# Linear attention and two MoE layers: eleven first products of block 1 moved into block 0, all stores issued by GpSimd, k, v and q in transfers of 512 KB, four weights converted ahead of block 0

## The chip, the cores and the metric

The kernel runs on one core of a Trainium2 chip. The metric is the device time of one execution in microseconds; the lower is the better. Times of runs are medians; the profile is of one further execution of the same program.

## What is computed

The reference is a linear attention with a root-mean-square norm, followed by two layers of two products each, in float32:

```python
kv  = einsum('bhsd,bhse->bhde', k, v)          # batch 8, heads 8, seq 576, head_dim 64
out = einsum('bhsd,bhde->bhse', q, kv)
x   = out / sqrt(mean(out * out, -1) + 1e-6) * g_norm
x   = x.transpose(0, 2, 1, 3).reshape(4608, 512)
h   = x @ w_in;  r = maximum(h, 0)             # 512 -> 2048
x   = (s * (r * r) + b) @ w_out                # 2048 -> 512
h   = x @ w2_in                                # second layer
y   = (h / (1 + exp(-1.702 * h))) @ w2_out
```

The weights arrive as 64-bit floats and are converted on the core, each into a high and a low float32r part; a product of float32 precision is then three products of 128x128 by 128x512 (high by high, high by low, low by high).

## The kernel before

The 4608 tokens are nine blocks of T = 512; the 512 features are four pairs of heads (NP = 4), two groups of two pairs (NG = 2). The 2048 hidden features are NF = 16 slices of 128. A weight tile is one slice of w_in (`which` 0) or of w_out (`which` 1), 512 KB as it arrives.

For one block j of attention, `kv_product` (L303) makes k'v of a batch on TensorE and `kv_keep` (L320) copies it out on ScalarE; `att_product` (L332) multiplies by q; `att_square` (L349) squares on ScalarE; for block 0 `att_mean`, `att_root`, `att_newton` work per pair of heads, for the other blocks `block_mean` (L392), `block_root`, `block_newton` work for all pairs at once, `y_store` and `y_load` (L410, L415) take the factor through memory to spread it over the partitions, and `att_scale` applies it. `att_split` (L428) makes the high part xh and the low part xl that the first layer reads.

The first layer, for the first three blocks (NPLAIN), is `mlp_h` (L473: twelve matmuls of 128x512, one slice f), `mlp_act` and `mlp_g` (the square of the positive part and its split into gh and gl), and `mlp_o` (L517: twelve matmuls that add slice f into four accumulators). I call such twelve matmuls a group, h(j, f) or o(j, f). The later blocks and the second layer use a scheme with seven products in place of eight (`g1_product`, `g2_product`), with sums of weights that are made once and stored to memory (`a_store`, `wo_store`, `op_store`).

A weight is loaded by `w_load` (L129) and converted in four steps: `w_low` (two ScalarE instructions), `w_words` (four on VectorE, L151 to L158), `w_hi` (one on ScalarE, L168) and `w_lo` (one on VectorE, L173). In block 0 every one of the 32 groups needs a weight of the first layer that has just been converted; blocks 1 and 2 use the same converted weights again.

The order is written by hand: each piece of work is put into a list by `at(slot, ...)`, where one slot is about one group of TensorE, the list is sorted by slot, and every engine gets its instructions in that order. So an instruction that waits holds up all that stands behind it on its engine. Loads and stores are issued by SyncE (SP), but for the `y` transfers, which GpSimd (POOL) issues; a queue too goes by its order. Large tiles come from 42 slots of 4 KB per partition (`big`), smaller ones from 23 of 2 KB (`mid`); PSUM has eight banks.

In the kernel before block 0 starts from a table and a formula for the conversions, and the blocks follow one another, h and o in turn:

```python
START = [(-61, -60, -54, -52, -45), (-59, -54, -53, -47, -42), ...]
weight(-128, -58.5, 3.5, CONV[0], 0, 0, 0)
weight(-89, -48.5, 4, CONV[0], 0, 1, 0)
for n, (f, w) in enumerate(...):
    weight(n - (5 if n < 12 else 4), n - 1, 1, CONV[1], 0, f, w)
for j in range(NPLAIN):
    plain(0, j, 32 * j, j == NPLAIN - 1)
```

## Time and profile before

| | |
|---|---|
| runs | 1566.7 us median of three, 1566.52 to 1568.53 |
| profiled execution, its own time | 1564.6 us |
| its span in the trace | 1562.8 us |
| mean granted TensorE clock | 0.992 of 2.4 GHz |
| busy: TensorE, weight loads | 1533.9 us (98%), 1235.5 us (79%) |
| busy: VectorE, ScalarE, GpSimd | 1063.9 us (68%), 795.4 us (51%), 40.3 us (3%) |
| DMA | 392.11 MB, 251 GB/s in the mean |

The profiled execution is 2.1 us below the median of the runs, and 1.8 us of its time lie outside the span. A matmul's busy time in the trace overlaps the next one's, so a busy TensorE is not one at its peak: how much it does is seen from the starts of its instructions. Names of engines in the rows: PE is TensorE, PEld its weight loads, DVE VectorE, ACT ScalarE, POOL GpSimd, SPq the queue of SyncE. A row of the timeline is start, duration, engine, line, operation, tiles and shape, number of instructions, and in brackets how long the engine had been idle before it and what ended that.

### The profile page before, as it was taken

How to read it: one execution, taken by the hardware profiler on the slowest of the kernel's cores; microseconds unless marked ns; L12 is line 12 of the kernel's file. 1: busy time of each engine (PE TensorE's matmuls, PEld its weight loads, DVE VectorE, ACT ScalarE, POOL GpSimd, SP SyncE). 2: the span in 40 equal slices, each digit the busy share in tenths (PEclk: the TensorE clock that was granted, in tenths of full speed). 3: DMA queues.
4: the chain of work that ended last, by engine and by line, in shares of the span. 5: the costliest groups of instructions: out<-in, count | busy, mean ns of one | idle time of the engine just before them, and what ended most of it. 6: DMA issues, size and time to landing. Idle time of an engine off the chain costs nothing.

```text
span 1562.8 us, 20560 instructions
## 1 busy us (share of the span) xinstructions
PE 1533.9 (98%) x7316; PEld 1235.5 (79%) x7316; DVE 1063.9 (68%) x1535; ACT 795.4 (51%) x1169; POOL 40.3 (3%) x84
## 2 busy tenths in 40 slices
PE   6999999999999999999999999999999999999998
PEld 4767777887788777888888888888888888888887
DVE  5997355566787468956761779678968896778422
ACT  4987455445696368934881335324522453244222
POOL 0010110101100011000000000000000000000000
PEclk8999999999999999999999999999999999999999
DMA  9463759869897889959770947884788478646670
GB/s 302 156 223 119 246 187 346 305 213 329 290 360 244 303 302 346 323 181 386 269 274 8 361 178 280 292 301 167 270 314 302 164 264 283 231 146 222 225 295 28
DMA packets 175527, 392.11 MB, mean 251 GB/s; under 512 B 23041, under 2 KB 54785, under 8 KB 175425
## 3 DMA queue, kind: packets, MB, share of 16 engines
q1 hardware_dynamic: 172096, 382.27, 69.7%
q0 software_dynamic: 3328, 8.52, 1.8%
q8 instruction: 58, 0.95, 0.2%
q14 instruction: 45, 0.36, 0.1%
HBM read 300.42 MB, written 90.31 MB: 250 GB/s over the span
## 4 chain that ended last, share of the span: by engine, by line
PE 84%; DVE 7%; issue 3%; DMA 3%; ACT 3%; SPq 0%; POOL 0%; DVEq 0%; ACTq 0%; POOLq 0%
PE o L524 26%; PE o L695 19%; PE h L481 8%; PE d L567 8%; PE a L567 8%; PE b L567 4%; PE f L567 4%; PE c L567 4%; DVE cu L157 1%; DVE w L173 1%; DMA yb<-yd 1%; PE kv L312 1%; DMA qq<-in_q 1%; PE o_ps L343 1%; DVE ca L158 1%
## 5 line engine op out<-in xcount | busy, mean ns | idle before, releaser
L524 PE MATMUL o<-gh,w 128*128 128x512 f32 x1280 | 406.8, 391 | 0.8 <-ACT gh L505 0.4
L524 PEld LDWEIGHTS o<-gh,w 128*128 128x128 f32 x1280 | 240.0, 188 | 56.6 <-issue 3.1
L695 PE MATMUL o<-gh,wl 128*128 128x512 f32 x896 | 276.5, 389 | 0.0
L524 PE MATMUL o<-gl,w 128*128 128x512 f32 x640 | 249.3, 390 | 0.4 <-DVE gl L514 0.2
L695 PEld LDWEIGHTS o<-gh,wl 128*128 128x128 f32 x896 | 168.2, 188 | 34.9
L481 PE MATMUL h<-xh,w 128*128 128x512 f32 x512 | 174.3, 402 | 4.0 <-DVE xh L442 2.7
L695 PE MATMUL o<-gl,wl 128*128 128x512 f32 x448 | 174.3, 389 | 0.0
L567 PE MATMUL d<-xh,wl 128*128 128x512 f32 x448 | 157.2, 391 | 7.0 <-DVE r L593 7.0
L567 PE MATMUL a<-xh,wl 128*128 128x512 f32 x448 | 157.5, 392 | 0.0
L524 PEld LDWEIGHTS o<-gl,w 128*128 128x128 f32 x640 | 120.1, 188 | 25.9 <-DVE gl L514 1.5
L481 PEld LDWEIGHTS h<-xh,w 128*128 128x128 f32 x512 | 98.1, 192 | 33.2 <-issue 3.5
L583 ACT ACTIVATE c<-a 128x512 f32<-128x512 f32 x56 | 33.4, 597 | 166.3 <-PE a L567 163.4
L567 PEld LDWEIGHTS d<-xh,wl 128*128 128x128 f32 x448 | 84.1, 188 | 27.8 <-DVE r L593 9.6
L481 PE MATMUL h<-xl,w 128*128 128x512 f32 x256 | 101.7, 397 | 0.0
L567 PEld LDWEIGHTS a<-xh,wl 128*128 128x128 f32 x448 | 84.5, 189 | 20.4 <-issue 1.9
L695 PEld LDWEIGHTS o<-gl,wl 128*128 128x128 f32 x448 | 84.1, 188 | 17.5
L638 DVE TENSOR_TENSOR gl<-r,gh 128x512 fp32r<-128x512 f32 x96 | 65.2, 688 | 39.0 <-PE o L524 23.1
L669 ACT ACTIVATE gh<-t 128x1024 fp32r<-128x1024 f32 x48 | 51.0, 1063 | 72.5 <-DVE t L660 62.4
L567 PE MATMUL a<-xl,wl 128*128 128x512 f32 x224 | 87.6, 391 | 0.0
L567 PE MATMUL d<-xl,wl 128*128 128x512 f32 x224 | 87.2, 389 | 0.0
L622 ACT ACTIVATE r<-r 128x1024 f32<-128x1024 f32 x84 | 84.6, 1052 | 0.0
L674 DVE TENSOR_TENSOR gl<-r,gh 128x1024 fp32r<-128x1024 f32 x64 | 77.3, 1221 | 6.9 <-ACT gh L669 6.9
(116 smaller groups left out, 2520.2 us busy)
## 6 DMA issues: line engine op xcount, KB each, us to landing
wl<-wsd SPq DMA_DIRECT2D x168, 512.0 KB, 7.0
wl<-wo2S SPq DMA_DIRECT2D x64, 512.0 KB, 5.7
wsd<-op SPq DMA_DIRECT2D x96, 256.0 KB, 4.7
w<-wod SPq DMA_DIRECT2D x48, 512.0 KB, 6.9
wl<-wo2A SPq DMA_DIRECT2D x48, 512.0 KB, 4.6
raw<-in_w_in SPq DMA_DIRECT2D x32, 512.0 KB, 7.9
raw<-in_w_out SPq DMA_DIRECT2D x32, 512.0 KB, 8.0
wl<-wsd SPq DMA_DIRECT2D x56, 256.0 KB, 6.3
```

The source lines that it names most:

```text
L157: dve.scalar_tensor_tensor(out=t, in0=raw[:, :, 1], scalar=SIGN_TOP, in1=t, op0=ALU.bitwise_and, op1=ALU.bitwise_or)
L158: dve.tensor_tensor(out=q, in0=t, in1=q, op=ALU.add)
L173: dve.tensor_sub(out=w[:, 1, :], in0=q.bitcast(F32), in1=w[:, 0, :].bitcast(F32))
L481: pe.matmul(h, lhsT=a, rhs=b, start=(n == 0), stop=(n == 3 * NP - 1))
L524: pe.matmul(acc[m, j][c], lhsT=a, rhs=x, start=(f == 0 and n == 0), stop=(f == NF - 1 and n == 2))
L567: pe.matmul(o, lhsT=a, rhs=b, start=(first and n == 0), stop=(n == 5), skip_group_check=not first)
L583: act.activation(st["c1"], st[0], AF.Copy)
L622: act.activation(R[q, n], R[q, n], fn)
L638: dve.tensor_sub(out=gl, in0=R[q, i][:, half, :], in1=gh.bitcast(F32))
L669: act.activation(hi, src, AF.Copy)
L674: dve.tensor_sub(out=lo, in0=src, in1=hi.bitcast(F32))
L695: pe.matmul(so[k, d], lhsT=a, rhs=b, start=(first and n == 0 and i == 0 and e == 0), stop=(n == 3 and i == 1 and e == 2), skip_group_check ...
```

## The change

The start is written out event by event (BEGIN), in place of START and its formulas. The first four slices of w_in (f 0 to 3) are loaded and converted there, and h(0, 0), h(0, 1) and h(0, 2) are cut in two: the half that needs the first two pairs of heads goes first (`mlp_h` has `first` and `last`). Dummy matmuls (`fill`) stand between them. `plan()` writes the order of the groups of blocks 0 to 2: eight h of block 0 first, then each o of block 0 followed by one h of block 0 or by one or two h of block 1, so that eleven h of block 1 stand in block 0; blocks 1 and 2 overlap likewise. The attention of block 1 moves to the start of block 0 (ATT). Weights are loaded 7.5 slots ahead of their group in place of 4 or 5 slots ahead of their conversion. All stores, the first q tiles, the constants and most of the tails of k and v (`tail_load`) are issued by GpSimd. k and v of a pair come in one transfer, q of a group in one transfer in place of two or four. `big` has 41 slots, `mid` 25.

```diff
-START = [(-61, -60, -54, -52, -45), (-59, -54, -53, -47, -42), (-54, -48, -48, -43, -41), (-50, -49, -46, -40, -36)]
-KV = ((1, 5), (20, 27), (34, 41), (46, 57), (62.5, 66.5), (74, 79), (84, 89))
-CONV = [(0, 1, 2, 3), (-0.5, 0, 1, 1.5)]
-NBIG, NMID = 42, 23
+KV = ((-0.5, 2.5), (24.5, 28), (34, 41), (46, 57), (62.5, 66.5), (74, 79), (84, 89))
+CONV = (-1.75, -1, 0.5, 1.0)
+BEGUN = 4
+LOAD = 7.5
+ATT = ((1.5, 2.5, 3.3), (40, 3.5, 4.8), (55, 4, 4.8), (67, 4, 4.8))
+LEAD_G = 3.9
+SIDE = (0, 0, 0, 1, 2, 0, 0, 0, 0, 2, 0, 1, 1, 1, 1, 2)
+BEGIN = [
+    (-0.1, 'tail', 0), (0.7, 'qp', 0, 0), (0.8, 'kv', 0, 0), (0.8, 'w', 0, 0, 0), (1, 'kv', 0, 1), (1.2, 'kv', 0, 2), (1.5, 'kv', 0, 3),
+    (1.6, 'w', 0, 1, 0), (1.7, 'w', 0, 2, 0), (1.8, 'w', 0, 3, 0), (2.0, 'qp', 0, 1), (6, 'kvp', 0, (0,), True, False), (6.25, 'fill', 2),
...
+    (25.8, 'hi', 0, 3, 0), (26.1, 'lo', 0, 2, 0), (26.1, 'lo', 0, 3, 0), (26.3, 'h', 0, 0, 0, 0, 2), (27.1, 'split', 0, 2),
+    (27.9, 'fill', 4), (28.3, 'split', 0, 3), (28.51, 'fill', 2), (28.71, 'fill', 4), (29.5, 'h', 0, 0, 1, 0, 2),
+    (32, 'h', 0, 0, 2, 0, 2),
+]
+def plan():
+    out = [("h", 0, f, *((2,) if f < 3 else ())) for f in range(8)]
+    ahead = 0
+    for i, n in enumerate(SIDE):
+        out += [("o", 0, i)]
+        if n:
+            out += [("h", 1, ahead + k) for k in range(n)]
+            ahead += n
+        else:
+            out += [("h", 0, 8 + sum(not k for k in SIDE[:i]))]
+    for i in range(NF - ahead):
+        out += [("o", 1, i), ("h", 1, ahead + i)]
...
+NBIG, NMID = 41, 25
     def wo_store(f):
-        nc.sync.dma_start(out=wod[f], in_=W[0, f, 1].bitcast(F32))
+        pool.dma_start(out=wod[f], in_=W[0, f, 1].bitcast(F32))
...
         for a, name in enumerate(OP_PAIRS[which][k]):
-            nc.sync.dma_start(out=op_place(m, i, which, name), in_=t[:, a, :].bitcast(F32))
+            pool.dma_start(out=op_place(m, i, which, name), in_=t[:, a, :].bitcast(F32))
...
     def kv_load(b, p):
-        kvin[b, p] = new2(F32, "k_in"), new2(F32, "v_in")
-        for n, t in enumerate(kvin[b, p]):
-            nc.sync.dma_start(out=t.rearrange("q (c d) -> q c d", c=4), in_=kv_h[b, p, :, n])
+        t = kvin[b, p] = new(big, [P, 2, 4, P], F32, "kv_in")
+        nc.sync.dma_start(out=t, in_=kv_h[b, p])
...
-    def q_load(j, g):
-        qin[j, g] = [new2(F32, "qq") for _ in range(2)]
-        for h, qq in enumerate(qin[j, g]):
-            for o, n, b, s in segments(j):
-                nc.sync.dma_start(out=qq[:, o:o + n], in_=q_h[b, g, :, h, s:s + n])
+    def q_load(j, g, queue=nc.sync):
+        qin[j, g] = new4(F32, "qq")
+        queue.dma_start(out=qin[j, g], in_=q_h[j, g])
...
-            nc.sync.dma_start(out=xd[0][j][p], in_=x)
+            pool.dma_start(out=xd[0][j][p], in_=x)
...
-    def mlp_h(m, j, f):
+    def mlp_h(m, j, f, first=0, last=NP):
...
-            nc.sync.dma_start(out=out[c * P:(c + 1) * P, j * T:(j + 1) * T], in_=t)
+            pool.dma_start(out=out[c * P:(c + 1) * P, j * T:(j + 1) * T], in_=t)
...
+    order = plan()
+    for n, (kind, j, f, *part) in enumerate(order):
+        slot = n - 0.005
+        if kind == "h":
+            at(slot, mlp_h, 0, j, f, *part)
+            at(slot + 1, mlp_act, 0, j, f)
+        else:
+            g = max(slot - LEAD_G, [e[:3] for e in order].index(("h", j, f)) + 1.01)
+            at(g, mlp_g, 0, j, f)
+            at(slot, mlp_o, 0, j, f)
...
+        if j == 0 and (kind == "o" or f >= BEGUN):
+            which = int(kind == "o")
+            at(n - LOAD, w_load, 0, f, which)
+            for i, fn in zip(CONV, (w_low, w_words, w_hi, w_lo)):
+                at(n - 4 + i, fn, 0, f, which)
...
-    for j in range(NPLAIN):
-        plain(0, j, 32 * j, j == NPLAIN - 1)
...
-    for j, slot in zip(range(1, NPLAIN + 2), (10, 35.5, 49, 66)):
-        attend(j, slot, 4, 4.8)
+    for j, slots in zip(range(1, NPLAIN + 2), ATT):
+        attend(j, *slots)
```

From the second slice of block 3's seven products on, the order on TensorE, VectorE and ScalarE is the same as before, instruction by instruction, but for some copies of block 2's sums, which stand a few places earlier; SP and POOL differ up to the end.

On TensorE, at the end of a group o(0, f) in block 0, before. A tile's number tells which one it is: xh_340 is block 0's operand, w_687 a weight converted just ahead.

```order
L524 MATMUL o_551<-gh_664,w_652 128x512
L524 MATMUL o_551<-gl_665,w_652 128x512
L524 MATMUL o_551<-gh_664,w_652 128x512
L481 MATMUL h_810<-xh_340,w_687 128x512
L481 MATMUL h_810<-xl_341,w_687 128x512
L481 MATMUL h_810<-xh_340,w_687 128x512 x2
L481 MATMUL h_810<-xl_341,w_687 128x512
```

The same engine with the change, at the end of o(0, 3). Here w_284 is the slice f 0 of w_in, already used for block 0, and xh_825 block 1's operand.

```order
L575 MATMUL o_769<-gh_851,w_862 128x512
L575 MATMUL o_769<-gl_852,w_862 128x512
L575 MATMUL o_769<-gh_851,w_862 128x512
L528 MATMUL h_964<-xh_825,w_284 128x512
L528 MATMUL h_964<-xl_826,w_284 128x512
L528 MATMUL h_964<-xh_825,w_284 128x512 x2
L528 MATMUL h_964<-xl_826,w_284 128x512
```

Before, every group of block 0 takes a new weight; now eleven groups that need no new weight stand between those that do.

On VectorE, in the start, before: the splits of pairs 1 to 3 (xh, xl) and the second weight's conversion.

```order
L442 CAST xh_340<-x0_331 128x512
L443 TENSOR_TENSOR xl_341<-x0_331,xh_340 128x512
L443 TENSOR_TENSOR xl_355<-x0_350,xh_354 128x512
L370 SCALAR_TENSOR_TENSOR y2_336<-ms_333,y2_336 128x512
L371 SCALAR_TENSOR_TENSOR y_335<-y2_336,y_335 128x512
L382 SCALAR_TENSOR_TENSOR x0_362<-o_ps_307,g_col_70,y_335 128x512
L173 TENSOR_TENSOR w_358<-ca_312,w_358 128x512
L443 TENSOR_TENSOR xl_355<-x0_362,xh_354 128x512
```

VectorE with the change, up to the splits of pairs 2 and 3 (that of pair 1 stands four rows ahead of the first).

```order
L217 TENSOR_TENSOR w_353<-ca_324,w_353 128x512
L195 TENSOR_SCALAR cu_350<-cu_350 128x512
L196 TENSOR_SCALAR cu_350<-cu_350 128x512
L201 SCALAR_TENSOR_TENSOR cu_350<-raw_212,cu_350 128x512
L202 ISA ca_349<-cu_350,ca_349 128x1024
L217 TENSOR_TENSOR w_370<-ca_345,w_370 128x512
L217 TENSOR_TENSOR w_383<-ca_349,w_383 128x512
L487 TENSOR_TENSOR xl_395<-x0_343,xh_394 128x512
L487 TENSOR_TENSOR xl_395<-x0_374,xh_394 128x512
```

The splits of pairs 2 and 3 now stand behind four converted weights, before behind two.

On GpSimd, the transfers of the factor y of block 5 (yd_143) and its neighbours, before.

```order
L412 DMA yd_142<-y 8x512
L418 DMA yb<-yd_142 64x512 x8
L412 DMA yd_143<-y 8x512
L418 DMA yb<-yd_143 64x512 x8
L412 DMA yd_144<-y 8x512
```

GpSimd with the change, around block 5's.

```order
L296 DMA wsd_0_104<-op 128x512 x4
L456 DMA yd_143<-y 8x512
L296 DMA wsd_0_104<-op 128x512 x2
L462 DMA yb<-yd_143 64x512 x2
L296 DMA wsd_0_104<-op 128x512 x2
L462 DMA yb<-yd_143 64x512 x4
L474 DMA x0d_125<-oc 128x512
L462 DMA yb<-yd_143 64x512 x2
L474 DMA x0d_125<-oc 128x512 x3
```

Stores of weights and of attention rows, which SP issued before, now stand in the same queue as the y transfers and among them. GpSimd issues 412 transfers in place of 72.

## Rows read from the trace of the kernel before

**Rows 1.** Busy time by stretch: window and length, busy and (count) of PE, PEld, DVE, ACT, POOL; PE clock, DMA share, GB/s.

```profile
27.60:46.20 18.60, 15.05 (x74) 10.38 (x73) 15.99 (x28) 14.03 (x26) 0.00 (x0) 0.72 0.85 302
46.20:80.90 34.70, 34.61 (x201) 25.91 (x200) 33.60 (x61) 32.64 (x58) 0.00 (x0) 1.00 0.44 137
80.90:93.10 12.20, 8.77 (x21) 4.29 (x21) 11.74 (x22) 12.04 (x22) 0.00 (x0) 0.72 0.90 282
121.60:139.30 17.70, 16.18 (x92) 10.76 (x91) 16.32 (x30) 15.94 (x29) 0.00 (x0) 1.00 0.21 64
605.00:1560.00 955.00, 953.36 (x4207) 789.07 (x4205) 654.44 (x841) 416.00 (x572) 0.00 (x0) 1.00 0.68 244
```

**Rows 2.** The chain that ended last, in order of time: start, length, what; block 2.

```profile
160.31 2.72 PE h L481 x12
```

**Rows 3.** Timeline of PE, 27 to 412 us.

```profile
27.63 0.90 PE L481 MATMUL h<-xh,w 128*128 128x512 f32 x1
...
46.24 0.39 PE L524 MATMUL o<-gh,w 128*128 128x512 f32 x1
...
49.06 1.15 PE L312 MATMUL kv<-v_in,k_in 128*64 128x64 f32 x32
...
50.36 0.50 PE L481 MATMUL h<-xh,w 128*128 128x512 f32 x1
...
80.91 1.05 PE L397 MATMUL ms<-sq,ones_c 128*32 128x512 f32 x4
84.82 1.05 PE L397 MATMUL ms<-sq,ones_c 128*32 128x512 f32 x2 [2.86 <-ACT sq L352]
...
93.16 0.39 PE L524 MATMUL o<-gh,w 128*128 128x512 f32 x1
...
121.67 0.39 PE L481 MATMUL h<-xh,w 128*128 128x512 f32 x1
...
137.54 0.39 PE L524 MATMUL o<-gh,w 128*128 128x512 f32 x1
...
411.71 1.06 PE L397 MATMUL ms<-sq,ones_c 128*32 128x512 f32 x8
```

**Rows 4.** Timeline of ACT in the start.

```profile
8.73 0.27 ACT L328 ACTIVATE kvs<-kv 64x128 f32<-64x128 f32 x1 [6.70 <-PE kv L316]
...
14.15 0.67 ACT L145 ACTIVATE cu<-raw 128x512 f32<-128x512 f32 x1
```

**Rows 5.** Timeline of DVE: first conversion, then the last step of weights.

```profile
14.85 0.43 DVE L151 TENSOR_SCALAR cu<-cu 128x512 f32<-128x512 f32 x1 [12.24 <-ACT cu L145]
...
44.92 0.68 DVE L173 TENSOR_TENSOR w<-ca,w 128x512 fp32r<-128x512 f32 x1
47.77 0.69 DVE L173 TENSOR_TENSOR w<-ca,w 128x512 fp32r<-128x512 f32 x1
51.23 0.69 DVE L173 TENSOR_TENSOR w<-ca,w 128x512 fp32r<-128x512 f32 x1
...
143.48 0.68 DVE L173 TENSOR_TENSOR w<-ca,w 128x512 fp32r<-128x512 f32 x1
```

**Rows 6.** Timeline of DVE and PE around block 5's factor y.

```profile
391.14 0.75 DVE L423 SCALAR_TENSOR_TENSOR oc<-oc,g_col,yb 128x512 f32<-128x512 f32 x1 [2.73 <-DMA yb<-yd]
401.84 0.50 PE L567 MATMUL d<-xh,wl 128*128 128x512 f32 x1 [2.04 <-DVE r L593]
```

**Rows 7.** Timeline of POOL there.

```profile
385.86 4.30 POOL L418 DMA_DIRECT2D yb<-yd  x8 [4.88 <-ACT cu L145]
```

**Rows 8.** The tile yb: count, duration in ns, least, median and most, first and last start.

```profile
L418 POOL DMA_DIRECT2D yb<-yd x64: 518/526/723, 99.2 to 597.1; - x64
```

**Rows 9.** DMA issues: count, KB each, median us from issue to landing.

```profile
out<-st SPq DMA_DIRECT2D x36, 256.0 KB, 2.5
yb<-yd POOLq DMA_DIRECT2D x64, 128.0 KB, 3.7
```

**Rows 10.** The end: SP's last stores.

```profile
1557.05 2.41 SPq L548 DMA_DIRECT2D out<-st  x4
```

More of the change, by code (lines that the diff above doesn't have):

```diff
@@ new lines, in plan @@
+def plan():
[10 more added lines that the diff above has]
+        out += [("o", 1, i), ("h", 1, ahead + i)]
+    done = 0
+    for i in range(NF - ahead, NF):
+        out += [("o", 1, i)]
+        if (NF - i) % 2:
+            out += [("h", 2, done)]
+            done += 1
+    for i in range(NF - done):
+        out += [("o", 2, i), ("h", 2, done + i)]
+    return out + [("o", 2, i) for i in range(NF - done, NF)]
@@ L211, in w_join, with w_spent @@
         dve.tensor_add(out=q.bitcast(F32), in0=w[:, 0, :].bitcast(F32), in1=w[:, 1, :].bitcast(F32))
+        w_spent(f)
+    spent = set()
+    def w_spent(f):
+        if f in spent:
+            drop(W.pop((0, f, 0)))
+        spent.add(f)
     sums, parts = {}, {}
@@ L309, in kv_product @@
                 for p in units:
[L310 to L311 removed]
+                    r = p % 2 * D
+                    kt_, vt_ = (kvin[b, p][:, n, c, h * D:(h + 1) * D] for n in range(2))
                     pe.matmul(kv[r:r + D, p // 2, h * D:(h + 1) * D], lhsT=kt_, rhs=vt_, start=(p in (opens, opens + 1) and h == 0 and c == 0), stop=False,
@@ L471 @@
     G, acc = {}, {}
-    def mlp_h(m, j, f):
+    def mlp_h(m, j, f, first=0, last=NP):
         x = xT[m, j]
-        h = G[m, j, f] = psum("h")
-        n = 0
-        for c in range(NP):
+        if first == 0:
+            G[m, j, f] = psum("h")
+        h = G[m, j, f]
+        n = 3 * first
+        for c in range(first, last):
+            assert m or (0, j, c) in done
             wh, wlo = (w_part(m, f, 0, i, c) for i in range(2))
@@ L482, in mlp_h @@
                 n += 1
-        if m or j == NPLAIN - 1:
+        if last < NP:
+            return
+        if m:
             drop(W.pop((m, f, 0)))
+        elif j == NPLAIN - 1:
+            w_spent(f)
         if f == NF - 1:
@@ L735, in at @@
         events.append((slot, len(events), fn, a))
-    def weight(load, slot, gap, conv_at, *unit):
-        at(load, w_load, *unit)
-        for i, fn in zip(conv_at, (w_low, w_words, w_hi, w_lo)):
-            at(slot + gap * i, fn, *unit)
-    def attention(slots, j, p):
-        at(slots[0], att_product, j, (p,))
-        for slot, fn in zip(slots, (att_square, att_mean, att_root, att_newton, att_split)):
-            at(slot, fn, j, p)
     def attend(j, slot, gap, late):
         for g in range(NG):
-            at(slot - 4 + g, q_load, j, g)
+            at(slot - 3.2 + g, q_load, j, g)
             at(slot + gap * g, att_product, j, (2 * g, 2 * g + 1))
@@ L875, in x_done, with start, fill @@
         drop(*(xin.pop(k) for k in left))
-    for p in range(NP):
-        at(-99 + p, kv_load, 0, p)
-        if p == 0:
-            at(-98.95, tail_load, 0)
-        at(START[p][0], kv_product, 0, (p,), p == 0, p == NP - 1)
-        at(START[p][0], kv_keep, 0, p)
-        at(-98.9 + p, q_half, p)
-        o, m, n, x = START[p][1:]
-        attention((o, m, m, n, x), 0, p)
-    weight(-128, -58.5, 3.5, CONV[0], 0, 0, 0)
-    weight(-89, -48.5, 4, CONV[0], 0, 1, 0)
-    for n, (f, w) in enumerate([(f - LAG * w, w) for f in range(1, NF + LAG) for w in range(2) if 0 <= f - LAG * w < NF][1:]):
-        weight(n - (5 if n < 12 else 4), n - 1, 1, CONV[1], 0, f, w)
+    warm = cp.tile([P, P], F32, name="warm")
+    idle = psum("idle")
+    def start(t, fn, *a):
+        at(t - 200, fn, *a)
+    def fill(n):
+        for _ in range(n):
+            pe.matmul(idle[:, :P], lhsT=warm, rhs=warm, start=True, stop=True)
+    for t, fn, *a in BEGIN:
+        start(t, {"fill": fill, "kv": kv_load, "q": q_load, "qp": lambda j, g: q_load(j, g, pool), "tail": tail_load, "w": w_load, "kvp": kv_product, "keep": kv_keep, "o": att_product,
+                  "sq": att_square, "mean": att_mean, "root": att_root, "newton": att_newton, "split": att_split, "low": w_low,
+                  "words": w_words, "hi": w_hi, "lo": w_lo, "h": mlp_h}[fn], *a)
+    start(60, drop, idle)
+    order = plan()
[8 more added lines that the diff above has]
+            at(slot, mlp_o, 0, j, f)
+            if j == NPLAIN - 1:
+                at(slot, wo_done, 0, f)
+            if f == NF - 1:
+                at(slot + 0.03, mlp_store, 0, j)
+        if j == 0 and (kind == "o" or f >= BEGUN):
[3 more added lines that the diff above has]
+                at(n - 4 + i, fn, 0, f, which)
     for b, slots in zip(range(1, B), KV):
@@ L987 @@
         act.add_instruction(mybir.InstLoadActFuncSet(name=nc.get_next_instruction_name(), act_func_set_id=6, ins=[], outs=[]))
-        warm = cp.tile([P, P], F32, name="warm")
         dve.memset(warm, 0.0)
-        idle = psum("idle")
-        for _ in range(14):
-            pe.matmul(idle[:, :P], lhsT=warm, rhs=warm, start=True, stop=True)
-        drop(idle)
+        fill(14)
         consts()
         for slot, _, fn, a in events:
+            if slot > STOP:
+                break
             fn(*a)
```

45 lines of the change are left out of this document (24 added, 21 removed).

## The prediction

> **What bounds the kernel now.** I read the windows first, since a busy share over the whole span mixes stages. From 605 to 1560 us TensorE is busy for 953.36 of 955.00 us at full clock [rows 1], and the chain of waits runs through groups of twelve matmuls that take 2.72 us each [rows 2]. The reader is to see that nothing can be gained there: the change leaves that work and its order as they are. So the question is how much TensorE loses before that, above all in block 0 (to 138 us), where each group needs a freshly converted weight.
>
> Busy time doesn't answer it, because a waiting TensorE can look busy; the starts of its instructions do [rows 3]. I set the time between two starts against the groups in between, at 2.72 us each [rows 2], and the product k'v, at 50.36 - 49.06 = 1.30 us [rows 3]. Three stretches lose time:
>
> - A, 27.63 to 46.24 us: 18.61 us for three groups (8.16) and a k'v: 9.15 us lost. The granted clock there is 0.72, a mean over full and half speed (2.4 and 1.2 GHz) [rows 1].
> - B, 80.91 to 93.16 us: 12.25 us for one group and sums of squares worth 1.06 (the row at 411.71): 8.5 us lost. The sums wait 2.86 us for ScalarE's squares [rows 3]; then matmuls run at the half clock, and the mean is again 0.72 [rows 1].
> - C, 121.67 to 137.54 us: 15.87 us for four groups (10.88) and a k'v: 3.7 us lost, at full clock [rows 1, 3].
>
> The cause of A and C is VectorE. One weight costs it 47.77 - 44.92 = 2.85 us; two weights in a row and the low part of a square take 51.23 - 44.92 = 6.31 us [rows 5], while TensorE's pair of groups that uses them takes 5.44 us. From 46.2 to 80.9 us VectorE is busy for 33.60 and ScalarE for 32.64 of 34.70 us [rows 1]. From its first conversion at 14.85 to the end of the last at 144.2 us VectorE has 129 us of work in line with the 32 groups of block 0 [rows 5]: it is the bound of this stage, and TensorE the follower.
>
> **The change, part by part.** The eleven groups h(1, f) cost TensorE nothing new: they are taken out of block 1. They do need block 1's attention sooner, which VectorE and ScalarE now do in the start. What they bring is time for conversions: 43 groups run while 32 weights are converted, so the ratio turns from 6.31 against 5.44 us per pair to about 6.31 against 7.31 (5.44 x 43/32).
>
> Start. Before, ScalarE makes the first low parts at 14.15 us though the copy of the first k'v had ended at 9.00 [rows 4]; now they stand right behind that copy. VectorE's first conversion may start at about 11.5 in place of 14.85 us [rows 4, 5], but two more weights are then converted ahead of the last splits, and the first h waits for splits of pairs 0 and 1. I set it at 26.5 in place of 27.63: **+1 us** of gain, between -1.5 (the extra conversions delay it) and +3 (it follows VectorE's 3.35 us).
>
> A. In place of whole groups, the halves of h(0, 0) to h(0, 2) on pairs 0 and 1 stand ahead, so that TensorE has 4 us of work while pairs 2 and 3 are split. VectorE's work up to the split of pair 3 is four weights less one step (11 us) and some 17 further operations of 0.6 to 0.75 us, 22 to 23 us in all; with the idle share of before (2.6 of 18.60 us [rows 1]) and waits on the first sums, it is done near 38 us. TensorE with its halves and a k'v from 26.5 would be there at 33 to 34. So 4 us of wait, and about 1.5 us at the half clock or between matmuls: 5.5 us lost in place of 9.15, **+3.6**, between 0 (nothing is better) and +9 (all goes).
>
> B. The sums of block 1 still stand some four slots behind the products whose squares they wait for, and ScalarE has the same queue ahead of it. I take half: 4 in place of 8.5, **+4.5**, between 0 and +8.5.
>
> C. At the last weight TensorE has 40 groups, four k'v and block 1's attention behind it: 26.5 + 108.8 + 5.2 + 3 = 144 us, while VectorE, started 3 us earlier, gets there at 141. So TensorE is the bound at the end, and of the 3.7 us I leave 1.7: **+2**, between 0 and +3.7.
>
> A new wait. The eleven groups do not stand evenly: up to o(0, 2) there are eight h in a row and then o and h in turn, each with a new weight, and h(1, 0) comes only behind o(0, 3). VectorE ends the 13th weight at 11.5 + 39 (13 weights of 2.85 and the words of the next) + 18 (three low parts, splits and factors of blocks 0 and 1, 0.6 to 0.75 us each) + 5 of idle time as before = 74 us. TensorE comes to that group at 26.5 + 32.6 (12 groups) + 2.6 (two k'v) + 3 (attention) + 9.5 (what A and B leave) = 74 us. That is even; I put **-1.5** there, between -6 (VectorE is a tenth slower than its sum) and 0.
>
> Stores. 340 transfers move from SP's queue to POOL's. POOL's own issues take 526 ns each [rows 8], so 340 x 0.53 = 180 us on an engine that is busy for 40 of 1563 us: hidden under TensorE, as buffers of stored tiles come free two slots or more before they are needed again. SP has fewer issues and may load earlier; TensorE waits for no load after the start, so 0. If that cover fails, the price is a load late by the length of a queue, some 2 us a piece. Only the last store shows: out<-st lands 2.5 us after issue from SP, yb<-yd 3.7 us from POOL [rows 9], and SP's last four start at 1557.05 [rows 10]. That is **-1.2**, between -2 and 0.
>
> One rule speaks against the stores on POOL. The rows show that 64 yb issues took between 518 and 723 ns, median 526, beside a VectorE that was busy for two thirds of the time [rows 8, 1]: at most 0.2 us of delay each. The Trainium skill ("SBUF — State Buffer", section "Who interferes with whom") says that a transfer issued by GpSimd has its descriptors written by GpSimd, which is shut out while VectorE runs a copy, cast or tensor_scalar in its two-port mode, and so advises another queue. By it each moved store could be held for up to the length of such an instruction; by the rows the hold is 0.2 us at most, 340 x 0.2 = 68 us of POOL's time, still off the path.
>
> k, v and q in fewer, larger transfers carry the same bytes: 0, with SP's saved issues in the same cover. The dummy matmuls fill waits; they can delay the h behind them by their own length, which is inside A's lower bound.
>
> From 139 to 605 us VectorE and TensorE lose some 11 us in the sums for the seven products; the order there is unchanged, and I set it at 0, between -17 (the third rival) and +2.
>
> Sum: 1 + 3.6 + 4.5 + 2 - 1.5 - 1.2 = 8.4 us gained on the profiled execution's own 1564.6: 1556.2. The median of the runs is 2.1 us above that execution, so the median after is about **1558**.
>
> **The rivals.** First, all waits of block 0 go: A's 9.15, B's 8.5 and C's 3.7, less the last store, 20 us at most and some 17 likely, 1549. For it speaks the slack of 43 groups against 32 weights; against it the sums of block 1, which are ordered as tightly as before.
>
> Second, VectorE remains the bound: the lead is used up by the 13th weight, and the waits of A and B come back there with a half clock behind them. It decides if VectorE's sum of 74 us is over by more than a tenth. Then the wait takes 6 us or more and the gain is under 3: 1565. The even finish of the two sums speaks for it, the easier end of block 0 against it.
>
> Third, slower: the y transfers stand behind stores in POOL's queue. Before, POOL waited 4.88 us for block 5's factor and then issued eight yb in 4.30 us [rows 7]; VectorE waited 2.73 us for one of them at 391.14, and TensorE 2.04 us for VectorE at 401.84 [rows 6]. With two stores ahead of each pair, at 0.53 to 1.06 us each [rows 8], pairs land 1.1 to 2.1 us later, some 4.2 us a block over four pairs, in four blocks: 17 us, 1575. It decides once yb lands later than VectorE arrives, and VectorE already waits. Against it: POOL's wait of 4.88 us leaves room for stores ahead of the factor, and later pairs land while VectorE works on the first. The skill's rule above would add to this rival's price and not create it.
>
> That the change doesn't do what it says is excluded by the order: the eleven groups stand where the text says.
>
> **How the numbers follow.** My forecast, 1553 to 1563, has a chance of 0.55; all waits gone 0.20; VectorE still the bound 0.15; slower 0.10. A measurement of this kernel can tell about 0.2%, 3.1 us, from no change, so "same" is 1563.6 to 1569.8. It takes most of the second rival; the third is all of "slower". Faster takes the forecast, the first rival and a little of the second: 0.77, 0.13, 0.10. The range runs from 1547 (first rival, with a better start) to 1566 (second rival); what it leaves out is the third and the outermost of the first.
>
> **What would show it.** In the timeline of TensorE, the first h at 26 to 27 us; three halves and then a wait of about 4 us; the sums of block 1 with a shorter wait ahead of them and less half clock; the stretches A to C together losing some 10 us less; no new wait of TensorE on VectorE between 70 and 86 us of over 3 us. The stretch 345 to 605 should lose no more than before, and VectorE's wait for yb stay near 2.7 us. The forecast is wrong if that wait grows in each block, if TensorE's waits in 60 to 90 us add up to more than before, or if the first h comes later than 29 us.

## The result, and the profile after

The change makes the kernel faster: 1548.04 us median of four runs (1547.74 to 1548.96) against 1567.62 us of four runs of before (1566.52 to 1568.84); ratio 0.9876, 95% interval 0.9859 to 0.9893. Beside the last experiments the changed kernel ran again (e16_after_again, expected at 1547 to 1549): 1548.41 against 1565.22 us, ratio 0.9890 (0.9874 to 0.9905). The gain is 17 to 20 us. I had forecast 8.4, with the right sign: 1548.0 lies below the forecast's own 1553 to 1563, near the lower end of the whole range of 1547 to 1566, and close to the first rival's 1549. Two single executions, one of e6_act_sp (3971.69 us) and the profiled one of e11_before_fill (2190.55 us), lie far above all others and are left out of what follows.

The profiled execution after took 1548.96 us, with a span of 1547.1. Busy time by stretch, same columns as [rows 1], its first four stretches and one more:

```profile
27.60:46.20 18.60, 16.60 (x145) 12.66 (x144) 17.51 (x32) 12.96 (x25) 0.00 (x0) 0.91 1.05 379
46.20:80.90 34.70, 34.49 (x165) 26.06 (x162) 33.51 (x61) 33.16 (x60) 6.92 (x12) 1.00 0.59 188
80.90:93.10 12.20, 12.20 (x55) 9.96 (x54) 11.36 (x20) 11.11 (x20) 0.00 (x0) 1.00 0.01 1
121.60:139.30 17.70, 17.70 (x109) 14.44 (x108) 13.03 (x22) 14.77 (x26) 7.29 (x11) 1.00 0.84 283
345.00:600.00 255.00, 251.55 (x1184) 197.76 (x1183) 186.76 (x316) 172.00 (x249) 71.40 (x132) 1.00 0.88 309
```

TensorE is full in the third and fourth stretch, where it was not, and its clock in the first and third is 0.91 and 1.00 in place of 0.72. VectorE and ScalarE are as busy as before from 46 to 81 us, where TensorE hardly waited for them in either kernel; the waits that shrank or went are those from 28 to 46, from 81 to 93 and from 122 to 139 us.

The timeline of TensorE after; a row is read as in [rows 3]:

```profile
27.45 0.47 PE L528 MATMUL h<-xh,w 128*128 128x512 f32 x1
30.15 0.50 PE L528 MATMUL h<-xh,w 128*128 128x512 f32 x1 [1.77 <-DVE xh L486]
31.63 3.83 PE L927 MATMUL idle<-warm 128*128 128x128 f32 x20
35.22 0.48 PE L528 MATMUL h<-xh,w 128*128 128x512 f32 x1
46.31 0.50 PE L528 MATMUL h<-xh,w 128*128 128x512 f32 x1
56.00 1.57 PE L441 MATMUL ms<-sq,ones_c 128*32 128x512 f32 x8
57.51 0.50 PE L528 MATMUL h<-xh,w 128*128 128x512 f32 x1
77.51 0.74 PE L528 MATMUL h<-xh,w 128*128 128x512 f32 x2 [0.21 <-DVE w L217]
257.69 0.50 PE L528 MATMUL h<-xh,w 128*128 128x512 f32 x1 [1.49 <-DVE st L586]
303.85 0.40 PE L360 MATMUL kv<-tail_v,tail_k 128*64 128x128 f32 x3 [0.91 <-DMA tail_v<-in_vt]
356.69 0.50 PE L618 MATMUL d<-xh,wl 128*128 128x512 f32 x1 [1.34 <-DVE r L644]
574.75 0.50 PE L618 MATMUL d<-xh,wl 128*128 128x512 f32 x1 [1.03 <-DVE r L644]
1541.61 0.39 PE L575 MATMUL o<-gh,w 128*128 128x512 f32 x1
```

The first eight rows are block 0: some 5 us up to 35 us in a wait and in the dummies (idle<-warm), then no wait over 0.3 us. The next two are waits that the change brought in. The next two have twins in before, as the order is the same there:

```profile
367.22 0.50 PE L567 MATMUL d<-xh,wl 128*128 128x512 f32 x1 [1.28 <-DVE r L593]
...
591.11 0.50 PE L567 MATMUL d<-xh,wl 128*128 128x512 f32 x1 [1.04 <-DVE r L593]
```

So the changed kernel is 367.22 - 356.69 = 10.5 us ahead at the first and 591.11 - 574.75 = 16.4 us at the second. Between them lie four blocks whose instructions on TensorE, VectorE and ScalarE stand in the same order, and they gave 5.8 us. VectorE's waits for yb fall there from 2.73, 1.39 and 3.08 us to a single one of 1.36. Behind the second twin row the two kernels take 971.7 and 972.3 us.

### The profile page after: what moved, and what is told of

The parts are those of the page before. It is cut to its first block, busy times and chain, and to the rows that moved or that the text cites. A ratio compares the mean times of both kernels' runs of the same rounds, so it can differ in the third digit from the quotient of the medians.

```text
span 1547.1 us, 20632 instructions
## 1 busy us (share of the span) xinstructions
PE 1528.4 (99%) x7368; PEld 1237.8 (80%) x7368; DVE 1062.8 (69%) x1535; ACT 789.4 (51%) x1169; POOL 231.8 (15%) x424
## 4 chain that ended last, share of the span: by engine, by line
issue 50%; PE 34%; ACT 5%; POOL 4%; DVE 3%; DMA 3%; SPq 0%; POOLq 0%; ACTq 0%; DVEq 0%
PE o L575 17%; PE h L528 5%; PE d L618 3%; PE a L618 3%; ACT r L673 1%; PE b L618 1%; PE f L618 1%; PE c L618 1%; DMA kv_in<-in_kv 1%; POOL out L599 1%; DMA x0d<-oc 1%; PE kv L356 1%; POOL yb L462 1%; PE o_ps L387 1%; DMA wsd<-op 1%
## 5 line engine op out<-in xcount | busy, mean ns | idle before, releaser
L528 PE MATMUL h<-xh,w 128*128 128x512 f32 x512 | 170.3, 394 | 3.5 <-DVE xh L486 1.8
L599 POOL DMA_DIRECT2D out<-st x36 | 19.5, 542 | 591.0 <-DVE st L768 467.4
```

Source lines behind the costliest of these rows:

```text
L528: pe.matmul(h, lhsT=a, rhs=b, start=(n == 0), stop=(n == 3 * NP - 1))
L599: pool.dma_start(out=out[c * P:(c + 1) * P, j * T:(j + 1) * T], in_=t)
```

## Experiments

Changed means the changed kernel, 1548.0 to 1548.4 us (0.9876 to 0.9890). Ratios are to runs of before on the same chip.

The twin rows can be found in every profile, and they tell where a kernel wins or loses. The start of the first, and the time from it to the second:

| kernel | first twin row at, us | from the first to the second, us |
|---|---|---|
| changed | 356.69 | 218.1 |
| before | 367.22 | 223.9 |
| e3_h1_behind | 368.84 | 218.0 |
| e1_stores_sp | 356.31 | 226.8 |
| e12_weights_sp | 353.36 | 231.3 |
| e6_act_sp | 356.49 | 221.8 |
| e5_before_pool | 370.93 | 227.7 |
| e13_before_pool_q | 367.79 | 227.0 |

The other nine variants of the changed kernel, itself run again included, take 218.0 to 218.8 us between the two.

### Where in block 0 the slack is needed

**e3_h1_behind**: the eleven h of block 1 right behind o(0, 15).

```diff
-    for i, n in enumerate(SIDE):
...
+    for i in range(NF):
+        out += [("o", 0, i)] + ([("h", 0, 8 + i)] if i < 8 else [])
+    ahead = sum(SIDE)
+    out += [("h", 1, f) for f in range(ahead)]
```

> The changed kernel with its eleven first products of block 1 moved from inside block 0 to right behind o(0, 15); start, stores and transfers as changed. Theory A, the slack of 43 groups against 32 weights makes the gain: 32 groups reach the last weight at 26.5 + 87 + 8 = 122 us while VectorE needs 141 us, so that TensorE waits some 15 to 19 us in block 0 and the time is 1560 to 1568, no better than before. Rival, the better start and the stores make it: under 4 us slower than 1548.

Measured: 1561.69 us, ratio 0.9965 (0.9952 to 0.9978). 13 us of the gain go, as theory A had it, near the lower end of its range: the slack is what block 0 gains from. The 5 us that are left don't come from the start: this kernel reaches the first twin row 1.6 us later than before, and makes its gain between the two, where it is as fast as the changed kernel. So the later gain doesn't need the eleven groups in block 0.

**e7_side_later** moves the first of the eleven by four groups, **e8_att_later** the attention of block 1 with it.

```diff
-SIDE = (0, 0, 0, 1, 2, 0, 0, 0, 0, 2, 0, 1, 1, 1, 1, 2)
+SIDE = (0, 0, 0, 0, 0, 1, 2, 0, 0, 2, 0, 1, 1, 1, 1, 2)
-ATT = ((1.5, 2.5, 3.3), ...
+ATT = ((5.5, 2.5, 3.3), ...          (e8_att_later alone)
```

> The changed kernel with the first h of block 1 four groups later (behind o(0, 5) in place of o(0, 3)), the same eleven in block 0. Two more of the new weights are then wanted before it. If VectorE's lead is used up at that point (my sum had both engines at 74 us), TensorE waits 2 to 4 us more for converted weights between 75 and 95 us: 1550 to 1552. If it has some 3 us of lead, no change, within 1.5 us of 1548.

> As e7_side_later, and the attention of block 1 four groups later too, so that its squares and sums stand in the stretch where o and h alternate and not in that of eight h in a row. Theory A, the sums waited before because ScalarE in the o and h stretch has the squares of the first layer and two new weights a pair ahead of them: a wait of 2 to 4 us at the sums of block 1 comes back, with matmuls at the half clock behind it, 4 to 9 us slower than e7_side_later. Rival, the squares were late only because the whole of block 0 ran behind VectorE: within 2 us of e7_side_later.

Measured: 1555.64 us, 0.9922 (0.9909 to 0.9936), and 1550.55 us, 0.9896 (0.9882 to 0.9911). TensorE's timeline in e7_side_later, its four waits between 76 and 93 us:

```profile
78.15 0.74 PE L528 MATMUL h<-xh,w 128*128 128x512 f32 x2 [0.44 <-DVE w L217]
82.87 0.73 PE L575 MATMUL o<-gh,w 128*128 128x512 f32 x2 [1.36 <-DVE w L217]
86.33 0.74 PE L528 MATMUL h<-xh,w 128*128 128x512 f32 x2 [0.44 <-DVE w L217]
90.42 0.50 PE L575 MATMUL o<-gh,w 128*128 128x512 f32 x1 [1.54 <-ACT w L212]
```

Four more new weights stand ahead of h(1, 0) here (f 11 and 12 of w_in, f 4 and 5 of w_out; the expectation counts two). They cost 3.8 us of waits for conversions, where the changed kernel waits 0.21, and the whole is 7 us slower, dearer than the expectation's 2 to 4. So both engines do reach this point together, as my two sums of 74 us said; the new wait was priced at 1.5 us and costs 0.2. In the later kernel my theory of the sums fell by half. A wait at the sums does come back, in TensorE's timeline of e8_att_later:

```profile
67.03 1.05 PE L441 MATMUL ms<-sq,ones_c 128*32 128x512 f32 x4
69.65 2.05 PE L441 MATMUL ms<-sq,ones_c 128*32 128x512 f32 x4 [1.57 <-ACT sq L396]
```

It costs 3 us, and not by the clock, which was granted at 1.00 from 69.65 to 71.6 us: two of the four sums wait for the third square, the other two for the fourth, which ends at 70.60. But the kernel is 5 us faster than e7_side_later, not slower: the attention's work, taken from VectorE and ScalarE before 80 us, leaves the conversions a lead, and the four waits are gone. Both sides of the expectation missed, since I counted the place of the sums and not whom the attention's work holds up.

ScalarE's timeline tells why the sums waited in before, and hardly do now. Before, the product of q for block 1's second two pairs starts at 76.9 us, and its two squares stand here:

```profile
80.65 0.63 ACT L168 ACTIVATE w<-ca 128x512 fp32r<-128x512 f32 x1 [0.55 <-DVE ca L158]
81.19 0.80 ACT L504 ACTIVATE r<-r,cst_sb 128x512 f32<-128x512 f32 x1
82.02 0.63 ACT L505 ACTIVATE gh<-r 128x512 fp32r<-128x512 f32 x1
82.56 0.65 ACT L144 ACTIVATE ca<-raw 128x512 uint32<-128x512 uint32 x1
83.11 0.66 ACT L145 ACTIVATE cu<-raw 128x512 f32<-128x512 f32 x1
83.68 0.61 ACT L168 ACTIVATE w<-ca 128x512 fp32r<-128x512 f32 x1
84.20 0.57 ACT L352 ACTIVATE sq<-o_ps 128x512 f32<-128x512 f32 x1
...
85.81 0.57 ACT L352 ACTIVATE sq<-o_ps 128x512 f32<-128x512 f32 x1
```

After, the product starts at 52.0 us and the squares at

```profile
54.90 0.58 ACT L396 ACTIVATE sq<-o_ps 128x512 f32<-128x512 f32 x1
55.38 0.61 ACT L212 ACTIVATE w<-ca 128x512 fp32r<-128x512 f32 x1
55.90 0.58 ACT L396 ACTIVATE sq<-o_ps 128x512 f32<-128x512 f32 x1
```

The same distance in slots is 8.9 us of ScalarE's queue in one place and 3.9 in the other. Between the product and its second square ScalarE works off thirteen other instructions before, and waits 0.45 and 0.55 us for VectorE; after, in the stretch of eight h, it has five and no wait.

**e15_att3** moves an attention by two groups (block 4's; the expectation calls it block 3's), with the output and the tails on SyncE as in e9_out_tail_sp below.

```diff
-ATT = (..., (67, 4, 4.8))
+ATT = (..., (65, 4, 4.8))
```

> The changed kernel with the stores of the output and the tails on SyncE (as e9_out_tail_sp) and the attention of block 3 two groups earlier. The wait of TensorE at 256 us (1.3 us; VectorE's copy of block 1's sums waits for the buffer of a stored x0d) goes: 1545 to 1546. If the wait only moves, 1546.8 as e9_out_tail_sp.

Measured: 1554.46 us, 0.9928 (0.9915 to 0.9940), 7 us slower than e9_out_tail_sp; both sides of the expectation missed. The wait at 256 us stays (1.16 us), and the moved sums wait 4.36 us for ScalarE, whose timeline shows for what:

```profile
264.33 0.60 ACT L396 ACTIVATE sq<-o_ps 128x512 f32<-128x512 f32 x1 [8.45 <-DMA x1d<-st]
```

The square wants the buffer of a block of x1d that GpSimd has not stored yet. So it is the buffers behind GpSimd's stores that bind here, and earlier work asks for more of them.

### Stores and queues

```diff
e1_stores_sp       all stores         - pool.dma_start(...)   + nc.sync.dma_start(...)
e12_weights_sp     wo_store, op_store, a_store alone, the same edit
e6_act_sp          x0d, x1d, output and tails, the same edit
e5_before_pool     kernel before, all stores   - nc.sync.dma_start(...)   + pool.dma_start(...)
e13_before_pool_q  as e5_before_pool, and q laid out as in the change, one transfer for each half of its tile
```

> The changed kernel (1548.0 us) with all its stores issued by SyncE again; the q tiles, constants and tails stay on GpSimd. Theory A, the gain is the order of block 0: the time stays within 1546 to 1549, as the stores were costed at nothing but the last one (a gain of 1.2 us), and the waits of GpSimd's queue at 256 us (1.5 us of TensorE behind a store of x0d) go. Theory B, part of the gain is that stores left SyncE's queue: the loads of SyncE wait behind stores that wait for their data, and TensorE loses 4 us or more between 345 and 600 us and some in block 0; 1552 to 1560.

> The changed kernel with the stores of weights and of their sums alone issued by SyncE again (176 transfers), those of activations and of the output on GpSimd. Theory, SyncE waits for VectorE's tile ahead of each such store (94 us in 33 waits when all stores are there) and its loads go out in bunches: most of the 7 us that all stores on SyncE cost, 1552 to 1555. Rival, the stores of activations make it: within 2 us of 1548.

> The complement: the stores of x0d, x1d and of the output, and the tails, issued by SyncE, those of weights on GpSimd. If the weights' stores are the ones that hold the loads up: 1546 to 1548, as the waits behind x0d at 256 us go as well. If the activations' are: 1550 to 1555.

> The kernel before (1566.4 to 1567.6 us) with all its stores issued by GpSimd, nothing else changed. Theory A, a store that waits for its tile holds up the loads behind it in SyncE's queue, they then go out in a bunch and the y transfers land late: the waits of TensorE on VectorE between 345 and 600 us shrink as they do in the changed kernel (by 4 to 6 us), and the time is 1560 to 1563. Rival, the gain there needs the other parts of the change: within 2 us of before.

> The kernel before with all stores issued by GpSimd (as e5_before_pool, which gained nothing) and q laid out so that it comes in two whole transfers per group in place of two to four pieces. Theory, the many short pieces of q load the engines of the transfers just as the y transfers are under way, and the stores' move and q's layout work together: 2 to 5 us faster than before. Rival, neither matters without the order of block 0: within 1.5 us of before.

Measured: all stores on SyncE 1555.2 us, 0.9921 (0.9907 to 0.9935); weights alone 1559.44, 0.9958 (0.9940 to 0.9975); activations, output and tails alone 1552.83 (three runs), 0.9916 (0.9894 to 0.9939). Before with its stores on GpSimd 1567.71, 1.0007 (0.9998 to 1.0016); with q's layout as well 1569.12, 1.0018 (1.0009 to 1.0028). So taking the stores back costs 4 to 11 us, most where those of the weights alone go back, and giving them to GpSimd in the kernel before gains nothing. In e1_stores_sp theory B held, in e5_before_pool the rival; in e13_before_pool_q both missed, and e12_weights_sp is dearer than either side had it. Both kinds of stores cost something, so e6_act_sp doesn't single out the activations'.

The table of the twin rows says where. In all three the first twin row comes no later than in the changed kernel, in e12_weights_sp 3.3 us sooner, as the waits at 257.69 and 303.85 us are gone; between the twins they lose 8.8, 13.2 and 3.7 us. In the kernel before, the same stretch gets 3 to 4 us longer with the stores on GpSimd. So in this stretch the move of the stores pays only together with another part of the change.

What happens is seen in the queues. SyncE waits for a tile ahead of its store, and what stands behind waits too. Two of its waits in e1_stores_sp (waited for, us in all, times, longest); in e12_weights_sp the second comes to 225.3 us in 61 waits:

```profile
SPq L596 <- ACT st L588: 108.9, 10, 44.4
SPq L296 <- DVE op L289: 94.4, 33, 10.1
```

Then the loads that were held go out together. SyncE's timeline around the factor y of block 7, in e12_weights_sp and with the change:

```profile
536.68 0.79 SPq L296 DMA_DIRECT2D wsd<-op  x2
...
539.39 2.55 SPq L307 DMA_DIRECT2D wl<-wsd  x5
```

```profile
523.95 13.43 SPq L307 DMA_DIRECT2D wl<-wsd  x5
543.62 0.94 SPq L177 DMA_DIRECT2D raw<-in_w_in  x2
```

In the first, five loads of weights go out in 2.6 us, just behind two stores, another load of weights and two of q; in the second, five in 13.4 us, and none from 537.4 to 543.6. What this does is seen at the factor y, which goes through memory, in GpSimd's timeline, with the change, then in e12_weights_sp, then before, where TensorE's wait that follows is shown too:

```profile
535.68 0.56 POOL L456 DMA_DIRECT2D yd<-y  x1 [4.49 <-DVE y L415]
538.44 1.06 POOL L462 DMA_DIRECT2D yb<-yd  x2 [2.21 <-issue]
```

```profile
539.14 0.56 POOL L456 DMA_DIRECT2D yd<-y  x1 [21.68 <-DVE y L415]
545.61 3.12 POOL L462 DMA_DIRECT2D yb<-yd  x6 [5.91 <-DMA yd<-y]
```

```profile
549.83 0.56 POOL L412 DMA_DIRECT2D yd<-y  x1 [122.53 <-DVE y L371]
556.25 4.27 POOL L418 DMA_DIRECT2D yb<-yd  x8 [5.86 <-PE f L567]
...
568.24 0.50 PE L567 MATMUL d<-xh,wl 128*128 128x512 f32 x1 [1.81 <-DVE r L593]
```

The windows of the 3 us behind yd in the first two of these profiles (columns as in [rows 1]; the last but one is the share of the transfers' engines):

```profile
535.68:538.68 3.00, 3.00 (x15) 2.49 (x14) 1.38 (x2) 3.00 (x5) 0.80 (x2) 1.00 0.70 229
```

```profile
539.14:542.14 3.00, 3.00 (x15) 2.49 (x14) 1.38 (x2) 3.00 (x5) 0.56 (x1) 1.00 1.04 391
```

The same place in seven profiles, gap worked out from the two starts:

| kernel | yd to first yb, us | DMA share in 3 us behind yd | TensorE's wait there, us |
|---|---|---|---|
| changed | 2.8 | 0.70 | none |
| before | 6.4 | 0.99 | 1.81 |
| e1_stores_sp | 7.1 | 0.96 | 2.53 |
| e5_before_pool | 5.8 | 0.96 | 6.23 |
| e13_before_pool_q | 5.9 | 1.00 | 6.17 |
| e12_weights_sp | 6.5 | 1.04 | 4.64 |
| e6_act_sp | 5.2 | 1.00 | 0.85 |

In these profiles, where the transfers' engines are full as y passes, yd takes about twice as long, and TensorE waits; in the changed kernel they are not, and it doesn't. How long it waits doesn't go by the gap alone: in e5_before_pool and e13_before_pool_q the yb behind it landed after 9.3 and 8.9 us in the median, before after 3.8. The link is shown at this place and by the moves of the stores; what fills the engines I followed in e12_weights_sp only. In e6_act_sp no load goes out from 532.3 to 547.6 us, and those of 518 to 528 take 10 to 14 us to land. After a long wait the clock falls: in e12_weights_sp TensorE's timeline goes on

```profile
560.27 0.79 PE L618 MATMUL d<-xh,wl 128*128 128x512 f32 x1 [4.64 <-DVE r L644]
560.86 0.63 PE L618 MATMUL d<-xl,wl 128*128 128x512 f32 x1
561.28 1.05 PE L618 MATMUL d<-xh,wl 128*128 128x512 f32 x2
```

with 0.63 us where full speed shows 0.39; the clock granted from 560.27 to 563.4 us is 0.50. In e5_before_pool the wait of block 5 did shrink (0.61 us in place of 2.04), but in block 7 six loads of weights and two of the raw weights went out around yd, and the gain was given back. Why SyncE comes to those loads at that moment in before and not in the changed kernel is open. The place of the eleven groups (e3_h1_behind), the dummies (e2_no_fill) and the size of the transfers of k, v and q (e10_kvq_halves) are not the other part that is needed, as the stretch stays at 218.0 to 218.8 us without any one of them. Left are the rest of the order in blocks 0 to 2, the slots of the weights' sums, and the number of buffers (42 and 41 large ones; a load goes when a buffer comes free); none of these was tried.

**e4_out_sp** and **e9_out_tail_sp** take the output's stores, then the tails too, back to SyncE.

```diff
-            pool.dma_start(out=out[c * P:(c + 1) * P, j * T:(j + 1) * T], in_=t)
+            nc.sync.dma_start(out=out[c * P:(c + 1) * P, j * T:(j + 1) * T], in_=t)
-        queue = pool if b else nc.sync
+        queue = nc.sync                       (e9_out_tail_sp alone)
```

> The changed kernel with the 36 stores of the output alone issued by SyncE again. If the last store costs what its queue takes to land it (median 5.9 us from GpSimd in the changed kernel, 2.5 us from SyncE before), the end comes 0.7 to 3.4 us earlier: 1544.6 to 1547.3. If the landing is set by the copies and the memory alone, no change, within 0.5 us of 1548.0.

> The changed kernel with the stores of the output and the loads of the tails of k and v issued by SyncE again, the other stores on GpSimd. The wait for tail_v (0.9 us at 303 us) and half a microsecond at the end go: 1546 to 1547. If the tails behind the loads of SyncE come no earlier, 1547.5 as with the output's stores alone.

Measured: 1547.52 us, 0.9872 (0.9855 to 0.9889), and 1546.82 us, 0.9869 (0.9856 to 0.9882). In the profile of e9_out_tail_sp the wait for tail_v is gone. Both medians are below the changed kernel's, by 0.5 to 1.6 us, but the intervals cover each other. In the profiles the stretch behind the second twin row is shorter than the changed kernel's 972.3 us, with 971.4 and 971.0, as an earlier end would have it; if a version beats it, it is e9_out_tail_sp. The first lies at the edge between its two expectations, the second in its range.

**e10_kvq_halves**: k, v and q in two transfers each.

```diff
-        nc.sync.dma_start(out=t, in_=kv_h[b, p])
+        for n in range(2):
+            nc.sync.dma_start(out=t[:, n], in_=kv_h[b, p][:, n])
```

> The changed kernel with k, v and q again in two transfers of 256 KB in place of one of 512 KB. As they carry the same bytes: no change, within 1.5 us of 1548. If the larger transfers brought something by the fewer issues of SyncE or a first product that starts earlier: 1549.5 to 1552.

Measured: 1549.57 us, 0.9894 (0.9875 to 0.9913): 1.2 to 1.5 us over the changed kernel, at the edge between the two expectations and within the interval. Inconclusive.

### The clock in the start

**e2_no_fill** leaves out all dummies of BEGIN, **e14_first_fill** all but the ten behind the first k'v; **e11_before_fill** puts ten into the kernel before.

```diff
-    (6.25, 'fill', 2), (6.61, 'fill', 8),                         (e2_no_fill alone)
-    (20.89, 'fill', 4), (24.7, 'fill', 2), (27.9, 'fill', 4), (28.51, 'fill', 2), (28.71, 'fill', 4),
+    at(-60.5, fill, 10)                                           (e11_before_fill)
```

> The changed kernel without the dummy matmuls in the start, but for the first fourteen. Theory A, the clock: after the wait of some 3.6 us at 31.6 us the matmuls of the first groups run at the half clock, as they did before from 31.66 to 40 us (0.60 to 0.73 us from start to start where full speed is 0.23); 2 to 4 us slower, 1550 to 1552. Rival: the wait there is set by VectorE's split and the dummies only fill it; no change, within 1 us of 1548.

> The changed kernel with only the first ten of its dummy matmuls in the start, those behind the first k'v; the later ones (ahead of and among the halves) left out. Theory, the first ten keep the clock of the start and the later ones that of the first groups: about half of the 4 us that all of them bring, 1549 to 1551, with the start at full clock (first h near 27.5 us) and the half clock in the first groups behind 31 us. Rival, the first ten do it all: within 1 us of the changed kernel.

> The kernel before (median 1566.4 to 1567.6 us, single runs from 1565.1 to 1572.0) with ten dummy matmuls behind the first product k'v, nothing else changed. Theory, the start of before runs at the half clock in a part of the executions (the first k'v of the start took 1.97 us from start to start in place of 0.98 in two profiles without the dummies, and the first h stood at 31.4 and 31.7 us in place of 27.5): the runs of 1568 us and more go, the median falls by 1 to 2 us and the first h stands at 27 to 28 us. Rival, the dummies only delay the first product of q by their own 2.4 us: 1 to 3 us slower.

Measured: 1551.92 us, 0.9902 (0.9888 to 0.9917); 1549.57 us, 0.9895 (0.9881 to 0.9908); 1566.34 us (eleven runs), 1.0001 (0.9989 to 1.0013). The windows from 12 to 27 us of the changed kernel, of e2_no_fill and of e14_first_fill:

```profile
12.00:27.00 15.00, 12.05 (x82) 6.14 (x83) 11.72 (x20) 12.33 (x24) 1.80 (x3) 1.00 1.07 371
```

```profile
12.00:27.00 15.00, 14.36 (x67) 7.19 (x68) 8.23 (x13) 7.33 (x15) 0.12 (x1) 0.56 1.07 380
```

```profile
12.00:27.00 15.00, 11.90 (x77) 5.71 (x77) 11.57 (x20) 12.34 (x24) 1.79 (x3) 0.99 1.07 372
```

Without the dummies that execution ran its start almost wholly at the half clock (0.56), a k'v was busy for 1.97 us in place of 1.15, and the first h stood at 31.70 us in place of 27.45. The time is in the range of theory A, but the wait at 31.6 us that it has in mind was not the place: the ten dummies behind the first k'v keep the start at 0.99 alone, while the later ones keep the first groups at full clock and take about as long as they save (in e14_first_fill the clock granted from 31 to 37 us is 0.50, and the next k'v starts at 37.96 us, in the changed kernel at 38.14). In time e14_first_fill isn't told apart from the changed kernel. In e11_before_fill ten dummies in the kernel before brought nothing that can be measured, as neither side had it; its only profile is the execution left out above.

The kernel before has the start without these dummies. Its profiled execution had the full clock in most of it (0.91 from 12 to 27 us), but the profile of e5_before_pool, whose start is the same code, shows 0.67 there and the first h at 31.41 us. I take it that some of the runs of before have that start. That is argued from e5_before_pool and from their spread (1565.5 to 1572.0 in twelve runs beside the first experiments, where the changed kernel's eight lie within 1.3 us), and e11_before_fill, which could have shown it, didn't.

## Why the prediction was wrong, and what it had right

On the profiled executions, 1564.6 and 1548.96 us, the gain is 15.6 where 8.4 was forecast. By its steps, what each forecast and what it gave:

- **Start**, forecast +1, gave +0.2: the first h stands at 27.45 in place of 27.63. The first conversion came at 12.30 and not 11.5 us, since ScalarE waited 2.56 us for the raw weight.
- **A**, forecast +3.6, gave +2.1: from 27.45 to 46.31 are 18.86 us for three groups, two k'v and a product of q (11.8), so 7.1 lost in place of 9.15. The split of pair 3 ended at 38.5, close to my 38. But three halves and then a wait, as I had it, didn't come: TensorE waited for the split of pair 1 (1.77 us) inside the first half and stood in dummies behind it, and at the splits of pairs 2 and 3 it didn't wait at all. In the profile of e16_after_again, the same kernel, the first h stands at 28.87 us and the first o at 63.51, here at 63.08: Start and A trade with each other, and their sum stays.
- **B**, forecast +4.5, gave +8: the sums take 56.00 to 57.51, half a microsecond more than they must. Mis-sized: I kept half the loss because the slots' distance is the same. It is, though not the "some four" slots of the text: the code puts the sums 1.4 slots behind the second products in both kernels. But ScalarE's queue is what counts, and it is short there.
- **C** and the **new wait**, forecast +2 and -1.5, gave +3.5: C is gone, the new wait is 0.2. e7_side_later shows that the new wait was real and how near it is.
- **Not foreseen**, -2.4: two waits of 1.49 and 0.91 us at 257.69 and 303.85, from stores and tails in GpSimd's queue (0.9 in all in e16_after_again). I had said that buffers come free in time; for x0d they don't.

This sums to some 11 us up to 355 us, by the twin rows 10.5, where the first five terms were forecast at 9.6. That this half came out near its sum is in part luck: errors of both signs met.

The step that failed is "**From 139 to 605 us ... I set it at 0**", with its ground, "SP has fewer issues and may load earlier; TensorE waits for no load after the start, so 0". It gave 5.8 us, above the bound of +2. The conclusion missed that a load can be late for nobody and still be in the way: in the changed kernel, released from the stores, SyncE's loads spread out, and the y transfers land while the engines have room; with the stores back on SyncE the stretch is 3.7 to 13.2 us longer. Which other part of the change this needs stays open, as the same move in the kernel before made the stretch longer. I had read the wait for yb [rows 6, 7], even as a rival in the other direction, and priced GpSimd's queue, but not what fills the engines as yd is under way. The third rival's mechanism, stores ahead of yb, is there (two stores between the pairs), and costs nothing where yd lands early. That the time is the first rival's 1549 is luck: its reason, that all waits of block 0 go, doesn't hold (7.1 us of A stay), and the stretch that it leaves out makes up for it.

The last store cost 0.6 us (5.45 us from the last matmul's start at 1541.61 to the end, 4.85 before), forecast 1.2. The medians gain more, 16.8 to 19.6, than the profiled executions' 15.6: I carried the 2.1 us that the profiled execution lies under the median over as a constant, while the one after lies 0.9 above its own. Part of the 2.1 may be the luck of its start (argued above, not shown).

Of GpSimd's stores the trace shows two sides. A yb issue took 534 ns in the median against 526 [rows 8] and no more than 743 ns, so the issues were not held. The prediction read the price of the stores' move off the issues alone, and it is the landing that shows it: out<-st landed after 5.9 us in the median in place of 2.5 [rows 9], x1d<-st after 7.1 in place of 2.7, though wsd<-op after 4.7 in both. Only the last stores and the two waits at 257 and 303 us pay for that. The Trainium skill ("SBUF — State Buffer", section "Who interferes with whom") has such transfers wait for their descriptors while VectorE runs certain copies; the later landing of two of these three fits that, though no run here separates it from other causes. The rule's advice would have cost 4 to 11 us in this kernel, by e1_stores_sp, e12_weights_sp and e6_act_sp.

## What to carry to other kernels

A queue whose issues wait for data (stores) can make those that follow go out in a bunch; where something small passes through memory on the critical path, look at the share of the transfers' engines at that moment and at what makes the bunch, not only at its own queue. When work is moved by slots, count what the engine that serves it has queued at the new place: the same distance was 3.9 us in one place and 8.9 in another. And before a profile is used as the sum's base, see whether its start, where waits and the clock vary, is that of most runs.

## What the runs showed of the hardware

- In these profiles a start with gaps between its matmuls ran at the half clock in some executions (0.56 and 0.67 granted from 12 to 27 us, e2_no_fill and e5_before_pool) and mostly at full clock in others (0.84 in e13_before_pool_q, 0.91 before); with ten dummy matmuls of 128x128 behind the first product it was at 0.95 to 1.00 in the thirteen profiles of the changed kernel and its variants.
- Behind waits of TensorE of 2.04 [rows 6] and 4.64 us (e12_weights_sp) matmuls ran at the half clock for some 3 us (0.50 granted from 403.3 to 406.5 and from 560.3 to 563.4 us); behind one of 1.34 us (356.69 in the profile after) they didn't (1.00 up to 360 us).
- The same store took 2.5 us to land from SyncE's queue and 5.9 from GpSimd's (256 KB, medians of 36), with issues of like length. Another, wsd<-op, took 4.7 us from either.
